# Three spectral products issued one gate/up product later in a float32 GLU plus spectral-filter kernel

## The chip, the cores and the metric

One NeuronCore of one Trainium2 chip runs the whole program. The metric is the device time of one execution in microseconds (us). The engines named below are TensorE (PE, with PEld for its weight loads), VectorE (DVE), ScalarE (ACT), GpSimd (POOL, nearly unused here) and SyncE (SP, whose queue issues almost all transfers).

## The reference

The input x has 2048 rows of 576 float32 values. It is normalised row by row, and the result is the sum of three terms:

```python
xn = _layernorm(x)                                   # per row, no scale or shift
A  = irfft2(rfft2(xn) * (w_r + 1j * w_i))            # 2-D over (2048, 576)
B  = (sigmoid(xn @ w_gate) * (xn @ w_up)) @ w_down   # 576 -> 4608 -> 576
out = x + A + B
```

All of it is wanted to nearly float32 accuracy.

## The kernel before, in words

TensorE multiplies operands that are rounded to a shorter float32 form. To keep the accuracy, the kernel cuts each operand in two parts: a high part, which is a rounded copy made by ACT, and a low part, the source minus the high part, made by DVE. A product is then three matmuls: high by high, low by high, high by low. This "rounding into two parts" stands ahead of every product.

**The GLU part.** The rows are worked in two pairs of 1024 (p = 0 and 1), and the 4608 hidden features in 36 blocks of 128. One block of one pair is a *unit* u. A unit computes gate and up for two row chunks by a seven-product scheme (the names A11, S1, T1 and so on are its sums). Each of the seven *gate/up products* (function `made`, issued by `prod`, L700) is seven matmuls of 128x128 by 128x512 into one of the PSUM banks pA, pB and pE. ACT and DVE empty those banks: L778 copies pA into pB, L785 and L791 copy pB to v, L788 and L796 apply the sigmoid. The down projection runs beside it, as groups of twelve (later six) matmuls of 128x288, tile ps (L1050), that DVE (L984) or ACT (L1032) adds to or copies into accumulators. The last blocks use tile po (L839) instead.

**The spectral part** runs inside the second pair, in three stages of 16 steps each; every step is a Python generator.

- `phase1b(t)`: product pd (14 matmuls, L527), a rounding of its result into ah and al (four ACT and four DVE instructions of 64x290, L535 and L536), product pa (6 matmuls, L542), a copy x1 to SBUF by ACT (L544), a store to DRAM.
- `phase2(i)`: a load x2, its rounding into x2h (ACT, L560) and x2l (DVE, L561), product pb (6 matmuls, L566), two swapped copies sw by ACT (L568, L569), the multiplication with the complex weight on DVE (L572 to L574), a rounding into zh (ACT) and zl (DVE), both by the helper `split` (L242, L243), product pc (6 matmuls, L582), a copy u by ACT (L584), a store.
- `phase3(t)`: a load u3, its rounding into uh (ACT, L603) and ul (DVE, L604), product py (6 matmuls, L609), copies, transposes pz (L622, L625), another rounding, product pe (12 matmuls, L640), and the addition of the result to the output rows. For t below 8 these rows are loaded into tile fin (L595) and stored from it (L653).

**What sets the order.** After each gate/up product the function `beside(i)` of the main loop advances the down projection by a piece (`rounds`) and then calls `aside()`, which advances every running generator by one `yield`. So one `yield` is one gate/up product. A table starts a phase1b step every 4.1 products, then a phase2 step every 4.1, then a phase3 step every 4.5 (U1, U2, U3). This gives the program order. From it a list scheduler makes, when the program is built, one fixed order for each engine and each queue, by its own estimates of when operands will be there; only instructions marked `keep_in_program_order` are held. On the chip every engine then works its own list from the front and waits where an operand or a buffer is not ready.

**Buffers.** pd, pa, pb, pc, py, pz, pe, ps and po all take their PSUM space from one pool of two buffers (`pair`, tag pp, two banks each). Banks pA and pB exist once, pE twice. ah, al, x2h, x2l, zh, zl, uh and ul have one buffer each; fin has two.

The main loop calls `aside` from `beside`:

```python
next(rounds, None)
turn(2 if u + 1 < NF else 1)
if u > NF + G:
    active.extend(b() for b in begin.pop(step, []))
    step += 1
    aside()
```

Of the kernel before, what the change touches and what calls it, by code (L numbers as in the profile page):

```python
# [163 lines left out]
def spectral_glu_kernel(ctx: ExitStack, tc: tile.TileContext, x, xt, xg, ri, w_in, w_down, out):  # L164
# [3 lines left out]
    def f32(ap):  # L168
        return ap.bitcast(F32)

    def load_r(dst, src):
        nc.sync.dma_start(f32(dst), src)
# [3 lines left out]
    def pair(name):  # L176
        return ps.tile([P, 2, 512], F32, tag="pp", name=name, bufs=2)
# [63 lines left out]
    def split(hi, lo, src, eng=None):  # L241
        nc.scalar.activation(hi, src, AF.Copy)  # L242
        (eng or nc.vector).tensor_tensor(lo, src, f32(hi), op=OP.subtract)  # L243
# [255 lines left out]
    def phase1b(t):  # L499
        pool, cf = R["pool"], R["cf"]  # L500
        xs = pool.tile([P, 2, KT + 1, P], F32, tag="xs", name=f"xs{t}", bufs=2)
        nc.sync.dma_start(xs.rearrange("p h k s -> p (h k s)"), xt[t])
        am = pool.tile([P, 2, 2, P], F32R, tag="am", name=f"am{t}", bufs=2)
        load_r(am, con["am"][:, t * 4 * P:(t + 1) * 4 * P].rearrange("p (a h m) -> p a h m", a=2, h=2))
        yield
        yield
        yield
        yield
        eo = pool.tile([P, 2, KT + 1, P], F32, tag="eo", name=f"eo{t}")
        tc.keep_in_program_order(nc.vector.tensor_tensor(eo[:, 1], xs[:, 0], xs[:, 1], op=OP.subtract))  # L510
        nc.vector.tensor_tensor(eo[:, 0], xs[:, 0], xs[:, 1], op=OP.add)
        fh = pool.tile([P, 2, KT + 1, P], F32R, tag="fh", name=f"fh{t}")
        fl = pool.tile([P, 2, KT, P], F32R, tag="fl", name=f"fl{t}")
        nc.scalar.activation(fh, eo, AF.Copy)
        nc.vector.tensor_tensor(fl, eo[:, :, :KT], f32(fh[:, :, :KT]), op=OP.subtract)
        r = slice(REM, 2 * REM)
        nc.vector.tensor_tensor(fh[r, :, KT], eo[r, :, KT], f32(fh[r, :, KT]), op=OP.subtract)
        yield
        yield
        pd = pair(f"pd{t}")  # L520
        for e in range(2):
            steps = []
            for k in range(2):
                steps += [(fh[:, e, k, :], cf[:, e, k, :]), (fl[:, e, k, :], cf[:, e, k, :]), (fh[:, e, k, :], cf[:, e, 2 + k, :])]
            steps.append((fh[:KR, e, KT, :], cf[:KR, e, 4, :]))
            for n, (l, r) in enumerate(steps):
                nc.tensor.matmul(pd[:, e, :NQ], l, r, start=n == 0, stop=n == len(steps) - 1)  # L527
        ah = pool.tile([P, 2, NQ], F32R, tag="ah", name=f"ah{t}", bufs=1)
        al = pool.tile([P, 2, NQ], F32R, tag="al", name=f"al{t}", bufs=1)
        for sl in range(2):  # L530
            for ci in range(2):
                o = slice(ci * N1, (ci + 1) * N1)
                i = slice(sl * N1, (sl + 1) * N1)
                v, r = pd[i, ci, :NQ], rstd[i, t:t + 1]
                nc.scalar.activation(ah[o, sl, :], v, AF.Copy, scale=r)  # L535
                nc.vector.scalar_tensor_tensor(al[o, sl, :], v, r, f32(ah[o, sl, :]), op0=OP.mult, op1=OP.subtract)  # L536
        yield
        yield
        pa = pair(f"pa{t}")
        for sl in range(2):  # L540
            for n, (h, m) in enumerate(((0, ah), (0, al), (1, ah))):
                nc.tensor.matmul(pa[:, sl, :NQ], am[:, sl, h, :], m[:, sl, :], start=n == 0, stop=n == 2)  # L542
        x1 = pool.tile([P, 2, NQ], F32, tag="x1", name=f"x1{t}", bufs=1)
        nc.scalar.activation(x1, pa[:, :, :NQ], AF.Copy)  # L544
        nc.sync.dma_start(sc1[2 * t * P:(2 * t + 2) * P].rearrange("(j p) n -> p j n", j=2), x1)

    def phase2(i):
        pool, bm, zz = R["pool"], R["bm"], R["zz"]
        kl = 2 * i
        x2 = pool.tile([P, 2, NQ], F32, tag="x2", name=f"x2{i}", bufs=2)  # L550
        nc.sync.dma_start(x2, sc1.rearrange("(p kl) n -> p kl n", kl=N2)[:, kl:kl + 2])
        w = pool.tile([P, 2, 2, NQ], F32, tag="ri", name=f"ri{i}", bufs=2)
        nc.sync.dma_start(w.rearrange("p a j n -> p (a j n)"), ri[i])
        wr, wi = w[:, 0], w[:, 1]
        yield
        yield
        yield
        h = pool.tile([P, 2, NQ], F32R, tag="x2h", name=f"x2h{i}")
        l = pool.tile([P, 2, NQ], F32R, tag="x2l", name=f"x2l{i}")
        tc.keep_in_program_order(nc.scalar.activation(h, x2, AF.Copy))  # L560
        nc.vector.tensor_tensor(l, x2, f32(h), op=OP.subtract)  # L561
        yield
        pb = pair(f"pb{i}")
        for j in range(2):
            for n, (k, m) in enumerate(((0, h), (0, l), (1, h))):
                nc.tensor.matmul(pb[:, j, :NQ], bm[:, k, :], m[:, j, :], start=n == 0, stop=n == 2)  # L566
        sw = pool.tile([P, 2, NQ], F32, tag="sw", name=f"sw{i}")
        nc.scalar.activation(sw[:N1], pb[N1:, :, :NQ], AF.Copy, scale=-1.0)  # L568
        nc.scalar.activation(sw[N1:], pb[:N1, :, :NQ], AF.Copy)  # L569
        z = pool.tile([P, 2, NQ], F32, tag="z", name=f"z{i}")  # L570
        t2 = pool.tile([P, 2, NQ], F32, tag="t2", name=f"t2{i}")
        nc.vector.tensor_tensor(z, wr, pb[:, :, :NQ], op=OP.mult)  # L572
        nc.vector.tensor_tensor(t2, wi, sw, op=OP.mult)
        nc.vector.tensor_tensor(z, z, t2, op=OP.add)  # L574
        zh, zl = zz[i % len(zz)]
        split(zh, zl, z)
        yield
        yield
        pc = pair(f"pc{i}")
        for j in range(2):  # L580
            for n, (k, m) in enumerate(((2, zh), (2, zl), (3, zh))):
                nc.tensor.matmul(pc[:, j, :NQ], bm[:, k, :], m[:, j, :], start=n == 0, stop=n == 2)  # L582
        u = pool.tile([P, 2, NQ], F32, tag="u", name=f"u{i}", bufs=2)
        nc.scalar.activation(u, pc[:, :, :NQ], AF.Copy)  # L584
        nc.sync.dma_start(sc2.rearrange("(p kl) n -> p kl n", kl=N2)[:, kl:kl + 2], u)

    def phase3(t):
# [14 lines left out]
        ul = pool.tile([P, 2, NQ], F32R, tag="ul", name=f"ul{t}")  # L602
        tc.keep_in_program_order(nc.scalar.activation(uh, u, AF.Copy))  # L603
        nc.vector.tensor_tensor(ul, u, f32(uh), op=OP.subtract)  # L604
        yield
        py = pair(f"py{t}")
        for sl in range(2):
# [493 lines left out]
    for (base, rate), phase, n in ((U1, phase1b, NT), (U2, phase2, N2 // 2), (U3, phase3, NT)):  # L1101
        for t in range(n):
            begin.setdefault(1 + base + int(t * rate), []).append(lambda t=t, phase=phase: phase(t))
# [458 lines left out]
```

## Time and profile before

| what | value |
|---|---|
| median of 3 runs | 1386.56 us (1386.12 to 1386.62) |
| the profiled execution | 1386.0 us |
| its span, first to last instruction | 1384.1 us |
| PE, share of the span | 99% (7688 matmuls) |
| PEld | 87% |
| DVE | 76% |
| ACT | 54% |
| granted TensorE clock | 1.000 |
| matmuls of pa, pc and py together | 288 |

The profiled execution is 1.9 us longer than its span, and 0.56 us below the median of the runs. The spectral stages lie at 697 to 897 us (phase1b), 915 to 1110 us (phase2) and 1110 to 1360 us (phase3) of the span. A row of a timeline gives start, duration, engine, line, operation, tiles, shapes and count, and in brackets the idle time of the engine before it with what ended it. A row of waits gives who waited for whom: the sum in us, how many times, the longest.

### The profile page before, as it was taken

What the parts mean: (1) busy time and instruction counts of PE and PEld (TensorE: products, weight loads), DVE (VectorE), ACT (ScalarE), POOL (GpSimd) and SP (SyncE); (2) the same over time, 40 slices, a digit from 0 to 9 for tenths busy, and PEclk for the clock granted to TensorE, in tenths of its full rate; (3) what the DMA queues carried; (4) which work ended last, traced back from release to release, by engine and by line L of the source; (5) the groups of instructions that cost most, each with busy time, mean ns of one, the idle gap of its engine ahead of it and who ended that gap; (6) DMA issues with size and microseconds to landing.
All of it is one profiled execution on the core that took longest, in us unless ns stands there. A gap on an engine that the chain in (4) does not pass through costs nothing. (4 is left out here: it accounts for less than half of the span.)

```text
span 1384.1 us, 20414 instructions
## 1 busy us (share of the span) xinstructions
PE 1371.5 (99%) x7688; PEld 1204.6 (87%) x7688; DVE 1046.0 (76%) x1523; ACT 742.0 (54%) x1180; POOL 3.3 (0%) x5
## 2 busy tenths in 40 slices
PE   8999999999999999999999999999999999999998
PEld 6888888888888888988888889988888889889888
DVE  7978889787878787999357467667767657777895
ACT  6644767777676777743155545445544434343432
POOL 0000000000000000000000000000000000000000
PEclk9999999999999999999999999999999999999999
DMA  7567776767667676686787767688888788676643
GB/s 256 207 252 285 269 313 263 274 265 272 261 258 264 247 264 247 262 271 221 258 260 232 220 211 239 199 276 271 270 269 268 234 259 256 216 238 184 195 149 86
DMA packets 120657, 337.05 MB, mean 244 GB/s; under 512 B 12560, under 2 KB 29744, under 8 KB 115824
## 3 DMA queue, kind: packets, MB, share of 16 engines
q1 hardware_dynamic: 119568, 334.44, 70.3%
q8 instruction: 61, 1.00, 0.3%
q10 hardware_dynamic: 992, 1.31, 0.3%
q14 instruction: 36, 0.29, 0.1%
HBM read 203.99 MB, written 131.71 MB: 243 GB/s over the span
## 5 line engine op out<-in xcount | busy, mean ns | idle before, releaser
L700 PE MATMUL pB<-X,w 128*128 128x512 f32 x1484 | 380.1, 393 | 0.6 <-ACT v L791 0.4
L1050 PEld LDWEIGHTS ps<-wf,hs 128*128 128x128 f32 x2436 | 348.0, 188 | 19.1 <-DVE acc L984 0.5
L1050 PE MATMUL ps<-wf,hs 128*128 128x288 f32 x2436 | 360.6, 295 | 0.1
L700 PEld LDWEIGHTS pB<-X,w 128*128 128x128 f32 x1484 | 269.2, 188 | 52.4 <-ACT v L791 3.3
L700 PE MATMUL pE<-X,w 128*128 128x512 f32 x1064 | 271.8, 392 | 0.0
L700 PE MATMUL pA<-X,w 128*128 128x512 f32 (+1 forms) x1006 | 256.4, 390 | 0.5 <-ACT X L476 0.2
L700 PEld LDWEIGHTS pE<-X,w 128*128 128x128 f32 x1064 | 194.1, 188 | 35.8 <-DVE ys L793 0.4
L700 PEld LDWEIGHTS pA<-X,w 128*128 128x128 f32 x1006 | 181.7, 188 | 34.1 <-ACT g L788 1.1
L971 DVE TENSOR_TENSOR hs<-ys,hs 128x1024 fp32r<-128x1024 f32 (+1 forms) x105 | 124.7, 1187 | 50.8 <-ACT hs L968 49.8
L968 ACT ACTIVATE hs<-ys 128x1024 fp32r<-128x1024 f32 (+1 forms) x105 | 108.0, 1028 | 48.4 <-PE ps L1050 41.7
L282 ACT ACTIVATE w<-raw 128x768 fp32r<-128x768 f32 (+1 forms) x106 | 100.3, 948 | 54.0 <-DVE raw L306 28.7
L815 DVE TENSOR_TENSOR ys<-ys,g 128x1024 f32<-128x1024 f32 x67 | 81.9, 1223 | 3.8 <-DVE ys L813 0.5
L284 DVE TENSOR_TENSOR w<-raw,w 128x512 fp32r<-128x512 f32 (+1 forms) x106 | 81.7, 771 | 2.5 <-ACT w L282 2.3
L793 DVE TENSOR_TENSOR ys<-v,pE 128x512 f32<-128x512 f32 x68 | 46.5, 684 | 44.0 <-ACT v L791 43.2
L796 ACT ACTIVATE g<-pB 128x512 f32<-128x512 f32 x68 | 40.5, 596 | 67.3 <-PE pB L700 67.2
L778 ACT ACTIVATE pB<-pA 128x512 f32<-128x512 f32 x68 | 39.6, 583 | 64.5 <-PE pA L700 64.4
L964 DVE TENSOR_TENSOR ys<-ys 128x1024 f32<-128x1024 f32 (+1 forms) x60 | 71.1, 1185 | 0.6
L839 PEld LDWEIGHTS po<-wb,hp 128*128 128x128 f32 x468 | 65.1, 188 | 2.6 <-ACT hp L877 0.4
L984 DVE TENSOR_TENSOR acc<-acc,ps 128x576 f32<-128x576 f32 x55 | 41.3, 751 | 34.2 <-PE ps L1050 33.9
L839 PE MATMUL po<-wb,hp 128*128 128x288 f32 x468 | 67.0, 295 | 0.0
L984 DVE TENSOR_TENSOR qs<-qs,ps 128x576 f32<-128x576 f32 x62 | 46.5, 750 | 25.2 <-PE ps L1050 25.1
L813 DVE TENSOR_TENSOR ys<-v,pE 128x512 f32<-128x512 f32 x67 | 45.8, 683 | 22.7 <-PE pE L700 22.1
(187 smaller groups left out, 1540.2 us busy)
## 6 DMA issues: line engine op xcount, KB each, us to landing
w<-wsp SPq DMA_DIRECT2D x246, 320.0 KB, 3.7
wsp<-w SPq DMA_DIRECT2D x34, 2240.0 KB, 7.2
wf<-fsp SPq DMA_DIRECT2D x105, 288.0 KB, 4.3
fsp<-wf SPq DMA_DIRECT2D x98, 288.0 KB, 3.4
raw<-in_w SPq DMA_DIRECT2D x34, 768.0 KB, 6.9
ri<-in_ri SPq DMA_DIRECT2D x16, 580.0 KB, 5.0
dt<-in_wd SPq DMA_DIRECT2D x32, 288.0 KB, 5.9
xs<-in_xt SPq DMA_DIRECT2D x16, 384.0 KB, 5.6
```

The costliest lines, as they stand in the source:

```text
L282: placed(nc.scalar.activation(o[:, :, :3, :], src, AF.Copy))
L284: placed(nc.vector.tensor_tensor(o[:, :, 3:, :], src[:, :, :KT, :], f32(o[:, :, :KT, :]), op=OP.subtract))
L700: strictly(nc.tensor.matmul(bank[:, cols], w[:, sw, :], X[:, x, sx, cols], start=start and j == 0, stop=stop and j == len(steps) - 1, skip ...
L793: nc.vector.tensor_tensor(y1, v[:, 1], bank["E"], op=OP.add)
L813: nc.vector.tensor_tensor(place(u, 0), v[:, 0], bank["E"], op=OP.add)
L815: nc.vector.tensor_tensor(h, h, g, op=OP.mult)
L839: nc.tensor.matmul(pd[b], l, r, start=start, stop=stop)
L964: nc.vector.tensor_tensor(o, at(a), at(b), op=op)
L968: nc.scalar.activation(hs[:, :, 0], o, AF.Copy)
L971: nc.vector.tensor_tensor(hs[:, :, 1], o, f32(hs[:, :, 0]), op=OP.subtract)
L984: nc.vector.tensor_tensor(o, a, b, op=op)
L1050: nc.tensor.matmul(pd[:, s], h[:, g, a, m], w[:, g, b], start=q == 0 and not seeded, stop=q == len(parts_) - 1, skip_group_check=seeded)
```

## The change

In each of the three phases one `yield` is added ahead of the product that stands behind a rounding, so that pa, pc and py are issued one gate/up product later than before, and what follows them in the same step moves along. Nothing is added or removed on any engine. The lines below the first edit have numbers higher by one, two or three in the changed kernel (L542 becomes L543, L582 becomes L584, L609 becomes L612).

```diff
@@ phase1b, behind the rounding into ah and al
         yield
         yield
+        yield
         pa = pair(f"pa{t}")
@@ phase2, behind split(zh, zl, z)
         yield
         yield
+        yield
         pc = pair(f"pc{i}")
@@ phase3, behind the rounding into uh and ul
         nc.vector.tensor_tensor(ul, u, f32(uh), op=OP.subtract)
         yield
+        yield
         py = pair(f"py{t}")
```

All engines keep their order up to the first pa. From there the scheduler's lists differ. Three places follow; the numbers behind the tile names only tell tiles of one name apart.

**TensorE, first step of phase1b (t = 0).** Before:

```order
L700 MATMUL pE_6422<-X,w_6055 128x512 x7
L700 MATMUL pB_6421<-X,w_6055 128x512 x7
L542 MATMUL pa_6476<-ah_6449,am_6359 128x290
L542 MATMUL pa_6476<-al_6450,am_6359 128x290
L542 MATMUL pa_6476<-ah_6449,am_6359 128x290
L700 MATMUL pA_6420<-X,w_6055 128x512 x3
L542 MATMUL pa_6476<-ah_6449,am_6359 128x290
L700 MATMUL pA_6420<-X,w_6055 128x512 x2
L542 MATMUL pa_6476<-al_6450,am_6359 128x290
L542 MATMUL pa_6476<-ah_6449,am_6359 128x290
L700 MATMUL pA_6420<-X,w_6055 128x512 x2
```

In the changed kernel:

```order
L703 MATMUL pE_6422<-X,w_6055 128x512 x7
L703 MATMUL pB_6421<-X,w_6055 128x512 x7
L703 MATMUL pA_6420<-X,w_6055 128x512 x7
L543 MATMUL pa_6497<-ah_6449,am_6359 128x290
L543 MATMUL pa_6497<-al_6450,am_6359 128x290
L543 MATMUL pa_6497<-ah_6449,am_6359 128x290 x2
L543 MATMUL pa_6497<-al_6450,am_6359 128x290
L543 MATMUL pa_6497<-ah_6449,am_6359 128x290
L703 MATMUL pB_6421<-X,w_6055 128x512 x7
```

The six matmuls of pa stood among the seven of a gate/up product; now they stand together behind it.

**TensorE, eleventh and twelfth step of phase2 (pc of step 10, pb of step 11).** Before:

```order
L700 MATMUL pE_9474<-X,w_6055 128x512
L582 MATMUL pc_9616<-zh,bmt 128x290
L700 MATMUL pE_9474<-X,w_6055 128x512 x6
L1050 MATMUL ps_7_5_0_9614<-wf_7_5_9432,hs_7_5_9543 128x288 x2
L582 MATMUL pc_9616<-zl,bmt 128x290
L582 MATMUL pc_9616<-zh,bmt 128x290 x2
L582 MATMUL pc_9616<-zl,bmt 128x290
L582 MATMUL pc_9616<-zh,bmt 128x290
L1050 MATMUL ps_7_5_0_9614<-wf_7_5_9432,hs_7_5_9543 128x288 x10
L700 MATMUL pA_9658<-X,w_6055 128x512 x7
L566 MATMUL pb_9673<-x2h_9652,bmt 128x290
L566 MATMUL pb_9673<-x2l_9653,bmt 128x290
```

In the changed kernel:

```order
L703 MATMUL pE_9474<-X,w_6055 128x512 x7
L1053 MATMUL ps_7_5_0_9614<-wf_7_5_9432,hs_7_5_9543 128x288 x12
L584 MATMUL pc_9642<-zh,bmt 128x290
L584 MATMUL pc_9642<-zl,bmt 128x290
L584 MATMUL pc_9642<-zh,bmt 128x290 x2
L584 MATMUL pc_9642<-zl,bmt 128x290
L584 MATMUL pc_9642<-zh,bmt 128x290
L703 MATMUL pA_9658<-X,w_6055 128x512 x7
L567 MATMUL pb_9673<-x2h_9652,bmt 128x290
L703 MATMUL pE_9660<-X,w_6055 128x512 x2
L567 MATMUL pb_9673<-x2l_9653,bmt 128x290
```

pc stands together behind the group ps, only one gate/up product (seven matmuls) ahead of the next pb; and pb, which was in one piece, now has two matmuls of pE behind its first.

**ScalarE, the same place.** Before:

```order
L242 ACTIVATE zh<-z_9571 128x580
L560 ACTIVATE x2h_9652<-x_9578 128x580
L796 ACTIVATE g_9470<-pB_9473 128x512
L584 ACTIVATE u_9623<-pc_9616 128x580
L778 ACTIVATE pB_9659<-pA_9658 128x512
```

In the changed kernel:

```order
L242 ACTIVATE zh<-z_9571 128x580
L799 ACTIVATE g_9470<-pB_9473 128x512
L586 ACTIVATE u_9649<-pc_9642 128x580
L561 ACTIVATE x2h_9652<-x_9578 128x580
L781 ACTIVATE pB_9659<-pA_9658 128x512
```

The rounding x2h of step 11 stood two places ahead of the copy u of step 10, which waits for pc; now it stands behind that copy. It does so in 14 of the 15 steps that follow another.

## The prediction

> **What bounds the kernel now.** I read the page first: the share of each engine, the clock, the chain that ended last.
>
> ```profile
> PE 1371.5 (99%) x7688; PEld 1204.6 (87%) x7688; DVE 1046.0 (76%) x1523; ACT 742.0 (54%) x1180; POOL 3.3 (0%) x5
> PEclk9999999999999999999999999999999999999999
> PE 45%; DVE 1%; ACT 1%; issue 0%; DMA 0%; ACTq 0%
> ```
>
> TensorE is the bound: 99% busy at full clock, and the chain that ended last is almost all PE. The change takes no matmul away, so it can only change the time in which PE stands still between matmuls. That the busy share leaves little room is not the whole story, because the row of a matmul covers its way through the array and overlaps the next one. A short standstill therefore hides inside "busy", and the starts must be read instead. So the next view is the timeline around one pa (step 5 of phase1b), and for comparison step 12:
>
> ```profile
> 757.22 1.77 PE L700 MATMUL pA<-X,w 128*128 128x512 f32 x7
> 762.00 1.30 PE L700 MATMUL pB<-X,w 128*128 128x512 f32 x5
> 763.19 0.65 ACT L1032 ACTIVATE qs<-ps 128x576 f32<-128x576 f32 x1
> 763.20 0.53 DVE L536 SCALAR_TENSOR_TENSOR al<-pd,rstd,ah 64x290 fp32r<-64x290 f32 x1 [0.56 <-ACT ah L535]
> 763.89 0.19 PEld L542 LDWEIGHTS pa<-ah,am 128*128 128x128 f32 x1 [1.02 <-ACT qs L1032]
> 763.89 0.40 PE L542 MATMUL pa<-ah,am 128*128 128x290 f32 x1 [0.60 <-ACT qs L1032]
> 764.13 0.29 PE L542 MATMUL pa<-al,am 128*128 128x290 f32 x1
> ...
> 848.12 1.79 PE L700 MATMUL pE<-X,w 128*128 128x512 f32 x7
> 852.97 0.29 PE L542 MATMUL pa<-ah,am 128*128 128x290 f32 x1
> 853.10 0.30 PE L542 MATMUL pa<-al,am 128*128 128x290 f32 x1
> 853.77 1.78 PE L700 MATMUL pA<-X,w 128*128 128x512 f32 x7
> 855.39 1.75 PE L1050 MATMUL ps<-wf,hs 128*128 128x288 f32 x12
> 856.97 1.30 PE L700 MATMUL pB<-X,w 128*128 128x512 f32 x5
> ```
>
> Undisturbed, seven gate/up matmuls take 855.39 - 853.77 = 1.62 us (0.23 each), a group ps 1.58, a matmul of pa 0.13. In step 5 five gate/up matmuls started at 762.00, so pa could have started at 763.15 and started at 763.89: 0.74 lost. Then the stalled matmul takes 764.13 - 763.89 = 0.24 where 0.13 is usual, another 0.11. Together 0.85, against an idle time of PEld of 1.02: the weight load runs ahead when nothing stops it, so a wait costs PE the idle time of PEld less about 0.15. With that rule the waits of PEld, by stage (697 to 737, 737 to 850, 915 to 1110 and 1110 to 1380 us), give the loss:
>
> ```profile
> PEld pa L542 <- ACT ah L535: 1.4, 3, 0.6
> PEld pa L542 <- DVE al L536: 0.3, 1, 0.3
> ...
> PEld pa L542 <- ACT qs L1032: 1.5, 3, 1.0
> PEld pa L542 <- PE ps L1050: 1.5, 3, 0.7
> PEld pa L542 <- DVE qs L984: 0.7, 1, 0.7
> PEld pa L542 <- issue: 0.5, 1, 0.5
> PEld pa L542 <- DVE al L536: 0.4, 1, 0.4
> ...
> PEld pc L582 <- DVE zl L243: 3.3, 11, 0.4
> PEld pc L582 <- ACT zh L242: 2.6, 9, 0.4
> ...
> PEld py L609 <- DVE acc L984: 0.7, 1, 0.7
> PEld py L609 <- DVE ul L604: 0.3, 1, 0.3
> ```
>
> pa: 6.3 us in 13 waits, so 6.3 - 13 x 0.15 = 4.4. pc: 5.9 in 20 waits, 5.9 - 3.0 = 2.9. py: 1.0 in 2 waits, 0.7. That is 8.0 us in all, and it is the most that the three edits can take away directly.
>
> **The change, part by part.** No instruction is added; the terms are waits that go, waits that stay and waits that come. The sum goes against the profiled execution, 1386.0 us; it lies 0.6 below the median of the three runs, 1386.56, and I add that at the end.
>
> *pa.* What pa waits for is late by its distance from pd. In step 5 pd ends where the next product begins, 757.22, and the last al ends at 763.20 + 0.53 = 763.73, 6.5 us later; this is the step with the greatest delay before pa (longest wait 1.0). In step 12 pd ends at 848.12 and pa starts at 852.97 without a wait, so there 4.85 is enough. The new list has three products between pd and pa in the steps 0 to 2 (3 x 1.62 = 4.9, and no ps there that loads ACT), three products and one ps in 3 to 9 (6.4), three and two ps in 10 to 15 (8.0). Only step 5 still misses, by about 0.1, and pays the 0.11 on top; I leave 0.3 for it and others like it. Gain 4.1. Behind pa nothing comes too early: the copy x1 and the next pd use the two PSUM buffers, and pd stands 1.6 (steps 11 to 15) to 3.2 us behind pa, where the copy of 128x580 takes 0.65. Bounds: 4.4 (all gone) and 1.8 (the waits on qs and ps, 3.7 in 7, stay; see the first rival).
>
> *pc.* The chain from pb to the parts of z, at step 10:
>
> ```profile
> 1034.92 1.78 PE L700 MATMUL pB<-X,w 128*128 128x512 f32 x7
> 1039.32 0.69 ACT L242 ACTIVATE zh<-z 128x580 fp32r<-128x580 f32 x1
> 1040.94 0.76 DVE L243 TENSOR_TENSOR zl<-z,zh 128x580 fp32r<-128x580 f32 x1
> 1042.62 1.48 PE L1050 MATMUL ps<-wf,hs 128*128 128x288 f32 x10
> 1042.82 0.66 ACT L584 ACTIVATE u<-pc 128x580 f32<-128x580 f32 x1 [1.75 <-PE pc L582]
> ...
> L560 ACT ACTIVATE x2h<-x 128x580 fp32r<-128x580 f32 x16 | 10.8, 677 | 0.0
> L561 DVE TENSOR_TENSOR x2l<-x,x2h 128x580 fp32r<-128x580 f32 x16 | 12.1, 758 | 5.8 <-ACT x2h L560 5.8
> ```
>
> pb ends at 1034.92, zh is there 5.1 us later and zl at 1041.70, 6.8 later. The new list puts pc three products and one ps behind pb (6.4) in most steps, 8.0 in some. zh is always in time. zl is needed one matmul later, at 6.4 + 0.13, and at a step as slow as this one would still be about 0.3 late. I take that for a quarter of the steps: 4 x (0.1 to 0.3 + 0.11) = 0.7 stays. Gain 2.2; bounds 2.9 and 1.0.
>
> *pb, the new wait.* The rounding x2h of the next step now stands on ACT behind u, which waits for pc. From the rows: pc ends at 1042.62 (the next matmul's start), u at 1042.82 + 0.66 = 1043.48, x2h would end at 0.68 more, 1044.16, x2l 0.76 after that, about 1044.95: 1.55 and 2.35 us behind pc. Queued behind x2h on ACT are the copies of the gate/up banks, and behind x2l on DVE the additions of ps, but both can run only when PE has gone on. Up to step 10 pb stands a product and a ps, 3.2 us, behind pc: hidden. In the steps 11 to 15 it is a single product, 1.62: x2h comes in the last moment, and x2l at 2.35 meets a matmul that, with the two or three fillers, is due at about 1.62 + 0.13 + 0.46 = 2.2, its weight load 0.13 sooner. I take 0.3 to 0.4 for each (0.2 late, 0.11 for the stalled matmul), 1.5 for five. Bounds: 0, if x2h starts as u ends and the fillers cover the rest; 4.3, if each costs what the worst wait of the trace cost, 0.85.
>
> *py and its followers.* Of 0.7 lost, 0.3 was for ul, now a product earlier and gone. The other wait was for a PSUM buffer that DVE empties in L984, and that meets py wherever py stands. pz and pe move along with new neighbours. I take a gain of 0.3; bounds +0.7 and -0.85 (one such wait more).
>
> *Queues.* The stores of x1 and u and those of fin move a product later on SP; the loads of w and wf stand around them. Their cover is worked out at the third rival; the sum takes zero.
>
> Sum: 4.1 + 2.2 - 1.5 + 0.3 = 5.1 us. 1386.0 - 5.1 = 1380.9 by the profiled execution, and with the 0.6 that the median stands above it 1381.5; the small waits beside pd (one of 0.5 us for fh) have a good chance to go with the others, so I say **1381.2 us**.
>
> **Rivals.** *A: the pairs are short, not the time.* Seven of the 13 waits of pa (qs 1.5 and 0.7, ps 1.5: 3.7 us) end with what empties or fills the two PSUM buffers, not with ah or al. If the new place of pa meets the same shortage, 3.7 - 7 x 0.15 = 2.6 us of the gain stays away: 1383.8. For it: the row of step 5, where L1032, not al, ends the wait. Against it: L1032 stands behind the four roundings on ACT there, so both end together, and both are past when pa comes 0.6 us later; steps 11 to 15 with the same two buffers have no wait at all. The Trainium skill (Perfetto Trace Analysis, Optimization Strategy) says that the same gap repeating on the engine that should be saturated can mean that there is too little PSUM for the next tile. By that rule it would come out like this rival; the trace bears it out in 7 of 13 waits.
>
> *B: pb takes back what pc gains.* If ACT or DVE is busy when pc ends (an hs copy of 1.0 us or its DVE partner of 1.2 us), each of the five late pb costs 0.85 instead of 0.3: 4.3 instead of 1.5, so 1381.2 + 2.8 = 1384.0. For it: in the old list x2h of those steps ran mostly ahead of pc. Against it: x2h follows u with nothing between, and two or three fillers stand there. The Trainium skill (PSUM — Partial Sum Buffer, Engine vs sequencer instructions) says that ScalarE's queue is strictly first in, first out, so that x2h cannot pass u; no row of this trace shows one passing another. Were it otherwise, the 1.5 would fall away and the sum would be 1379.7.
>
> *C: slower, by the SP queue.*
>
> ```profile
> 1195.36 0.38 SPq L653 DMA_DIRECT2D out<-fin  x1
> 1199.00 0.32 SPq L595 DMA_DIRECT2D fin<-spill  x1
> 1199.41 0.86 SPq L947 DMA_DIRECT2D wf<-fsp  x2
> ...
> 1215.49 1.79 PE L1050 MATMUL ps<-wf,hs 128*128 128x288 f32 x12
> ...
> DMA to landing us min/median/max: 2.7/3.6/5.1
> ...
> SPq L595 <- DMA out<-fin: 9.0, 6, 2.2
> ```
>
> The load of fin waits for the store of the fin two steps earlier, and everything behind it on SP waits with it. That store now comes a product and a ps (3.2 us) later, so the six waits could grow from 9.0 to 28 us. The wf behind one of them is issued at 1199.41, lands by about 1204 and is used two items later, at the earliest at 1215.49: 11 us of cover. Slower it gets from the point where a wait on SP is longer than that; each of the six would then hold PE for what is over. At 2.2 us over (the longest of these waits) it costs 13: 1394. The waits would have to grow fivefold, which is why I give it little.
>
> *D: no difference.* The standstills reappear elsewhere: PE's list is fixed, pA and pB are single banks, and new neighbours make new waits on their copies. Then 1386, from 8.0 gained and about 8 new.
>
> **How the numbers follow.** Forecast, 1379 to 1383.5: 0.68. A: 0.13. B: 0.10. C: 0.03. D: 0.06. What a measurement of this kernel can tell from no change is about 0.2%, 2.8 us, so faster means below 1383.8. The forecast lies below it, A and B on the line, half each side: faster 0.68 + 0.11 = 0.79; same 0.12 + 0.06 less 0.01 for a D that ends beyond = 0.17; slower 0.04. Range: the lower end takes all 8.0 gone and pb at 0, 1386.56 - 8.0 = 1378.5, the upper reaches over A and B, 1384.5.
>
> **What would show it.** In the profile after: the PEld waits of pa fall from 6.3 to below 1 us and those of pc from 5.9 to below 2; the matmul rows of pa stand as one block with distances of 0.13; a new row of PEld pb waiting for ACT x2h or DVE x2l, with 4 to 8 waits and 1 to 2.5 us, in the last third of phase2; PE, its matmul count and the clock as before. If the waits of pa on qs and ps stay, it was A; if the row of pb shows over 4 us, B; if ps waits for a DMA of wf, C. The prediction is wrong if the time is above 1384.5 or below 1378.5, and in its reasons if the gain does not sit at 697 to 850 us (about 4) and 915 to 1110 (about 1).

## The result and the profile after

The changed kernel takes **1378.93 us** (median of 6 runs, 1378.50 to 1379.43) against 1386.57 for the kernel before in the same session: ratio 0.9946, 95% interval 0.9933 to 0.9958. That is 7.6 us faster. The prediction said 1381.2, with a range from 1378.5 to 1384.5; the time lies inside it, 0.4 us above its lower end. The execution profiled below took 1378.5 us, with a span of 1376.5.

First the page of the changed kernel: the engines and the clock.

```profile
PE 1365.8 (99%) x7688; PEld 1205.7 (88%) x7688; DVE 1045.7 (76%) x1523; ACT 743.1 (54%) x1180; POOL 3.3 (0%) x5
PEclk9999999999999999999999999999999999999999
```

The matmul count and the clock are as before and PE's share still says 99%, as the prediction had warned: the 7.6 us do not show in it. They show in the starts. The first matmul of pd (step 0), of pb (step 0) and of pb (step 15), and the first of the last group, stand at the same places of PE's order in every kernel of this document. From the timelines of before (first four rows) and after (last four):

```profile
700.80 0.30 PE L527 MATMUL pd<-cf,fh 128*128 128x290 f32 x1
917.90 0.30 PE L566 MATMUL pb<-x2h,bmt 128*128 128x290 f32 x1
1091.45 0.29 PE L566 MATMUL pb<-x2h,bmt 128*128 128x290 f32 x1
1378.61 0.97 PE L839 MATMUL po_B<-wb,hp 128*128 128x288 f32 x6
...
700.82 0.29 PE L527 MATMUL pd<-cf,fh 128*128 128x290 f32 x1
912.90 0.30 PE L567 MATMUL pb<-x2h,bmt 128*128 128x290 f32 x1
1084.13 0.30 PE L567 MATMUL pb<-x2h,bmt 128*128 128x290 f32 x1
1371.01 0.95 PE L842 MATMUL po_B<-wb,hp 128*128 128x288 f32 x6
```

Three stages follow by subtraction. Stage 1 (first pd to first pb) took 217.1 us and now takes 212.1: 5.0 gained. Stage 2 (first pb to last pb) took 173.6 and now takes 171.2: 2.3 gained (173.55 less 171.23). The rest took 287.2 and now takes 286.9: 0.3. Of the 7.6 us, 7.3 lie in the first two.

The waits of PE's weight loads after, at 697 to 905, at 905 to 1110 and (py and pe only) at 1110 to 1380 us:

```profile
PEld pB L703 <- ACT v L794: 0.6, 1, 0.6
PEld pd L527 <- DVE fl L515: 0.2, 1, 0.2
...
PEld pb L567 <- DVE x2l L562: 1.4, 5, 0.3
PEld pc L584 <- DVE zl L243: 0.3, 1, 0.3
...
PEld pe L643 <- DVE z3l L243: 0.8, 2, 0.4
PEld pe L643 <- ACT z3r L633: 0.6, 2, 0.4
PEld py L612 <- DVE acc L987: 0.5, 1, 0.5
PEld py L612 <- DVE qs L987: 0.2, 1, 0.2
...
PEld pe L643 <- issue: 0.2, 1, 0.2
```

No wait of pa is left, where there were 6.3 us in 13. One wait of pc is left, where there were 20. The row of pb is new, with as many waits as predicted and at the small end of what was predicted for their sum. The timeline around step 5 of phase1b shows pa as the prediction wanted it, six matmuls with distances of 0.13 and no bracket of idle time (rows of DVE first, then PE):

```profile
759.95 0.53 DVE L536 SCALAR_TENSOR_TENSOR al<-pd,rstd,ah 64x290 fp32r<-64x290 f32 x1
...
754.84 1.77 PE L703 MATMUL pA<-X,w 128*128 128x512 f32 x7
761.20 0.29 PE L543 MATMUL pa<-ah,am 128*128 128x290 f32 x1
761.33 0.30 PE L543 MATMUL pa<-al,am 128*128 128x290 f32 x1
```

pd ends at 754.84, the last al at 760.48, pa starts at 761.20: the operand is 0.7 us early. Before, in this step, it was there 6.5 us behind pd; now 5.64, because DVE's order changed with it: before, an eo (0.55 us) stood ahead of the first al and a part of fh (0.41 us) ahead of the second, and now both come later.

### The profile page after: what moved, and what is told of

The parts are those of the page before. It is cut to its first block, busy times and chain, and to the rows that moved or that the text cites. A ratio compares the mean times of both kernels' runs of the same rounds, so it can differ in the third digit from the quotient of the medians.

```text
span 1376.5 us, 20419 instructions
## 1 busy us (share of the span) xinstructions
PE 1365.8 (99%) x7688; PEld 1205.7 (88%) x7688; DVE 1045.7 (76%) x1523; ACT 743.1 (54%) x1180; POOL 3.3 (0%) x5
## 4 chain that ended last, share of the span: by engine, by line
PE 91%; DVE 7%; issue 1%; ACT 1%; DMA 0%; DVEq 0%; ACTq 0%
PE pB L703 23%; PE ps L1053 22%; PE pE L703 16%; PE pA L703 15%; PE po L842 5%; PE pd L527 2%; PE pe L643 2%; PE pb L567 1%; PE py L612 1%; PE pc L584 1%; PE pa L543 1%; DVE acc L851 1%; DVE w L284 0%; PE pz L625 0%; PE b L1129 0%
```

## The experiments

The theory: **a product waits because its rounded operand is late, and one gate/up product more is enough**; behind pc the new order on ACT takes a little back at pb. The rivals are those of the prediction, above all A (two PSUM pairs are short). Each run is compared with the kernel before on the same chip (1386.52, 1386.73 and 1386.38 us in three sessions). The table gives medians of 5 runs (6 in its first row, 11 for pc alone and for the two runs with pd early), and the three stages of each profiled execution.

| kernel | median us | less than before | stage 1 | stage 2 | rest |
|---|---|---|---|---|---|
| before | 1386.57 | | 217.1 | 173.6 | 287.2 |
| changed kernel, run again | 1378.74 | 7.6 | 212.0 | 171.2 | 286.9 |
| pa alone | 1381.31 | 5.2 | 212.0 | 173.8 | 286.7 |
| pc alone | 1384.05 | 2.5 | 217.0 | 171.5 | 286.8 |
| pa and pc, not py | 1378.59 | 7.9 | 212.0 | 171.2 | 287.0 |
| pd early, from step 1 | 1384.18 | 2.3 | 214.8 | 173.9 | 286.7 |
| pd early, from step 3 | 1384.09 | 2.6 | 214.8 | 173.9 | 286.8 |
| changed, pa two later | 1381.25 | 5.5 | 213.7 | 171.4 | 286.8 |
| changed, pc two later | 1379.77 | 7.0 | 212.0 | 171.7 | 286.8 |
| changed, x2 earlier | 1378.09 | 8.6 | 212.0 | 170.4 | 286.8 |
| the same, py as before | 1378.14 | 8.2 | 212.0 | 170.4 | 287.0 |
| x2 earlier, pe later | 1377.30 | 9.1 | 212.1 | 170.4 | 286.0 |

The start of the first pd, which none of these edits moves in PE's order, varies from 700.6 to 702.6 us between these executions; that is why differences below 1 us are read in the stages.

### One edit at a time

The first two kernels have one of the three added lines each, the third has two.

```diff
+        yield
         pa = pair(f"pa{t}")
```

> Only pa stands one product later; pc and py as before. The theory of late operands (pa waits only because ah and al are not there yet): all of the gain at 697 to 897 us, about 5.0 of the 7.6 us, so 1386.6 - 5.0 = 1381.6; the 13 waits of PEld at pa (6.3 us) gone, the waits at pc as before (about 5.9 us in 20). The rival that the gain comes from the rearranged list as a whole, not from pa's own waits: less than half of it here, above 1383.5.

> Only pc stands one product later. The theory: pc's waits fall from 5.9 us in 20 to about 0.3 in 1, and x2h, now behind u on ScalarE, makes about 5 waits of pb with 1.4 us; net gain 2.2 us, 1384.4. The rival that pb takes back what pc gains: 1386, no difference. That both would add up with the run of pa alone to the whole change (less about 0.5 for py) is part of the theory.

> pa and pc one product later, py as before. The theory that py is worth 0.3 to 0.5 us: 1379.3, slower than the whole change (1378.9) by that little. The rival that the move of py costs (new waits of py on accumulators, pz and pe with new neighbours): 1378.4 or less, faster than the whole change.

pa alone: 1381.31 us, ratio 0.9963 (0.9951 to 0.9976). pc alone: 1384.05, 0.9982 (0.9973 to 0.9991). Their gains of 5.2 and 2.5 add up to 7.7; both together gave 7.9, and all three edits 7.6. So the parts are independent, and the place of the gain is as the theory had it: in the table each edit shortens its own stage, and the others stay within 0.5 us. The waits at 905 to 1110 us, with pa alone (first two rows) and with pc alone:

```profile
PEld pc L583 <- DVE zl L243: 3.5, 11, 0.5
PEld pc L583 <- ACT zh L242: 2.9, 10, 0.4
...
PEld pb L566 <- DVE x2l L561: 1.6, 5, 0.4
PEld pc L583 <- DVE zl L243: 0.3, 1, 0.3
```

21 waits of pc against one, and the five waits of pb come with the edit at pc. On py neither theory was confirmed: without its edit the time was 1378.59 where 1379.3 was the one expectation and 1378.4 or less the other; the ranges of the runs overlap (1378.36 to 1379.41 without, 1378.50 to 1379.43 with).

### Late operands or short pairs

This kernel leaves pa at about its old place and puts everything ahead of it in the step one product earlier. (The place is not quite the same: in step 5 pa now follows the group ps directly, where five matmuls of pB stood between.)

```diff
+        if t:
+            yield
         pa = pair(f"pa{t}")
...
-            begin.setdefault(1 + base + int(t * rate), []).append(lambda t=t, phase=phase: phase(t))
+            begin.setdefault(1 + base + int(t * rate) - (phase is phase1b and t > 0), []).append(lambda t=t, phase=phase: phase(t))
```

> pa stays where it was before among its neighbours (the same ps ahead of it), and everything ahead of it in the step (loads, sums, rounding, pd) is issued one product earlier from step 1 on, so the distance from pd to pa is that of the changed kernel. Late operands: the waits of pa go just as with pa moved, but for step 0, which is left as it was: about 0.3 us less gain than with pa moved alone, 1381.9. Two PSUM pairs short at pa's old place: the waits of pa on qs and ps (3.7 us in 7, 2.6 us of time) stay, 1384.3 or above. pd may wait for its own rounding if the load of xs is late: then PEld waits at pd beyond the 0.5 us of before, and the time says less.

1384.18 us: by the time alone this is the rival's number (1384.3 or above), not the 1381.9 of late operands. But the caveat of the expectation came true in part: a load of xs was late, though the wait that it made was at pa and not at pd. The worst wait of pa, of step 1, in the timeline (rows of DVE, ACT, PE):

```profile
718.93 0.56 DVE L511 TENSOR_TENSOR eo<-xs 128x384 f32<-128x384 f32 x1 [1.18 <-DMA xs<-in_xt]
719.52 0.52 DVE L536 SCALAR_TENSOR_TENSOR al<-pd,rstd,ah 64x290 fp32r<-64x290 f32 x1
...
720.08 0.50 ACT L535 ACTIVATE ah<-pd,rstd 64x290 fp32r<-64x290 f32 x1 [2.24 <-DVE al L536]
...
720.63 0.40 PE L544 MATMUL pa<-ah,am 128*128 128x290 f32 x1 [1.41 <-ACT ah L535]
```

An addition eo of step 2 waited 1.18 us for the load of xs; behind it on DVE stood an al of step 1, the last ah waited for that, and pa for the ah. From 737 us on no wait of pa was left. The same edit from step 3 on (`t > 2` in both places) keeps the first loads out of it:

> As the run with pd issued earlier, but only from step 3 on, so that the first loads of xs, which were late there, stay as before. Late operands: in steps 3 to 10 the kernel before lost 3.3 us at pa; all of it goes though pa keeps its old neighbours, 1386.5 - 3.3 = 1383.2, and no wait of PEld at pa is left at 745 to 850 us. Two PSUM pairs short at pa's old place: the waits on qs and ps, which lie in these steps, stay with 2.6 us, 1385.8.

1384.09 us, ratio 0.9983 (0.9974 to 0.9991): 2.6 gained, nearer to 3.3 than to 0.7. What decides is the stretch from 755 to 850 us (steps 5 to 10), where before every wait of pa is put down to what fills or empties the pairs. Before, its waits of PEld at pa:

```profile
PEld pa L542 <- PE ps L1050: 1.5, 3, 0.7
PEld pa L542 <- ACT qs L1032: 1.3, 2, 1.0
PEld pa L542 <- DVE qs L984: 0.7, 1, 0.7
```

With pd early there is none in this stretch, and PEld's only wait in it is one of pB (0.5 us). So 3.5 us of waits went by an earlier pd, and what rival A forecast, that they stay, has fallen. It does not follow that pa had waited for its operand. Step 7 of the kernel before (rows of DVE, then PEld):

```profile
785.69 0.51 DVE L536 SCALAR_TENSOR_TENSOR al<-pd,rstd,ah 64x290 fp32r<-64x290 f32 x1
...
788.36 0.53 DVE L536 SCALAR_TENSOR_TENSOR al<-pd,rstd,ah 64x290 fp32r<-64x290 f32 x1 [0.56 <-ACT ah L535]
788.96 0.19 PEld L542 LDWEIGHTS pa<-ah,am 128*128 128x128 f32 x1 [0.67 <-PE ps L1050]
```

The first three matmuls of pa read the halves of ah and al that the first two roundings write; the second of them ended at 786.20. But the first weight load of pa started only 0.07 us behind the fourth al. That one writes the other half, and it is the last to read pd, whose two PSUM banks pa gets in this step. So pa waited for a pair, and the roundings themselves empty it; the "PE ps" of the row had ended before. Steps 4, 8 and 9 show the same 0.07. In steps 3, 5, 6 and 10 pa gets the banks of the group ps ahead of it, and its first load started 0.05 to 0.06 us behind the end of qs, which empties them. In all eight steps the operands of its first three matmuls had been there for 1.8 us or more. These eight waits are 4.1 us of PEld. The other five (2.1 us, in steps 0 to 3) came at the fourth or fifth matmul and ended 0.05 us behind an ah or al: those are late operands.

The run with pd early cannot separate the two, because the same roundings that make the operand empty pd's pair. It also changes which pair is taken: in steps 4 to 10 pa now always gets that of pd. What a third pair would have saved was not measured.

Two steps did not follow: at 745 to 850 us the one wait of pa is

```profile
PEld pa L544 <- DVE al L536: 0.4, 1, 0.4
...
748.44 1.22 DVE L973 TENSOR_TENSOR hs<-ys,hs 128x1024 fp32r<-128x1024 f32 x1
749.69 0.53 DVE L536 SCALAR_TENSOR_TENSOR al<-pd,rstd,ah 64x290 fp32r<-64x290 f32 x1
750.27 0.40 PE L544 MATMUL pa<-ah,am 128*128 128x290 f32 x1
```

That is step 4. pd ended at 741.96 there, so al was still not there 8.2 us later, because DVE's order put an hs ahead of it. Step 3 lost 0.5 us, too, where the profile names no releaser; its last al ended at 738.21 and pa started at 738.31. Together the two steps lost 0.95 us by the starts, and with them the 2.35 us that stage 1 gained (217.1 to 214.75) would be the 3.3 of the expectation. So the distance from pd is the measure only as long as DVE's and ACT's orders stay the same.

### One more product

```diff
         yield
+        yield
         pa = pair(f"pa{t}")
```

> The changed kernel with pa one more product later, right ahead of the next pd. The theory that one product made pa's operands early enough: nothing left to gain, 1378.9 within 0.4, no waits of pa. The rival that pa's place, not the time behind pd, was what mattered: another difference of 1 us or more, in either sign; if pa and pd back to back run out of PSUM pairs, new waits of pd on x1 or of ps on al, 0.3 to 0.85 each in up to 15 steps, 1383 or more.

1381.25 us (1380.73 to 1381.46): 2.3 slower than the changed kernel. By the stages it is 1.8, of which 1.6 in stage 1; 0.7 more lies ahead of the first pd of the profiled execution (701.5 against 700.8), where the edit changes nothing. pa has no wait, but pd, now right behind it, has new ones (737 to 850 us):

```profile
PEld pd L527 <- ACT x L546: 1.7, 2, 1.0
PEld pd L527 <- ACT qs L1036: 0.7, 4, 0.2
...
PE pd L527 <- DVE qs L988: 0.6, 1, 0.6
```

x1 (shown as x) and qs empty the pairs. At the two longest of these waits (at 755.15 and 831.88) the last to end was DVE's addition of ps (L988), 0.12 us ahead of the load. So here, too, the pairs are short, now at pd. It cost less than the 1383 that the expectation gave for this rival, as only two steps lose more than 0.3 us at pd by the starts (0.55 and 0.83). For pc the second product has the same sign:

> The changed kernel with pc one more product later: it now stands beside the next pb, with 1 to 7 matmuls between them, and x2h is back ahead of u in most steps. Theory of late operands: pc's last 0.4 and pb's 0.7 go, 1377.8. The rival that the pairs are short: pb and pc hold both, so that the next ps or pb waits for u or sw, 0.3 to 0.85 in ten steps or more, 1382 to 1387.

1379.77 us (1379.39 to 1379.84). pc's last wait went, as expected, but pb, now beside it, has more:

```profile
PEld pb L567 <- issue: 2.1, 8, 0.4
PEld pb L567 <- DVE x2l L562: 0.6, 2, 0.3
PEld pb L567 <- DVE qs L988: 0.2, 1, 0.2
```

The theory's 1377.8 missed, and so did the rival's 1382: by the starts pb lost 1.9 us here against 0.7 in the changed kernel, and pc gained back 0.4; stage 2 is 0.5 longer. (In the profiled execution 1.1 us more lies ahead of the first pd, 702.0 against 700.8, where the edit changes nothing.) Two of the waits are for x2l. For eight of the nine others the profile names nothing, but DVE's rows show what ended them. The first of them, in step 1:

```profile
924.57 0.76 DVE L988 TENSOR_TENSOR qs<-qs,ps 128x576 f32<-128x576 f32 x1 [0.91 <-PE ps L1054]
...
925.44 0.19 PEld L567 LDWEIGHTS pb<-x2h,bmt 128*128 128x128 f32 x1 [0.22 <-issue]
```

In all nine DVE's addition of ps, which empties the pair that pb gets, ended 0.05 to 0.12 us ahead of the load, and x2h had been there for 1.2 us or more. So here as well the wait is for a pair.

### pb and x2h

The steps of phase2 from 1 on begin one product earlier, and pb is held where it was:

```diff
         yield
+        if i:
+            yield
         pb = pair(f"pb{i}")
...
-            begin.setdefault(1 + base + int(t * rate), []).append(lambda t=t, phase=phase: phase(t))
+            begin.setdefault(1 + base + int(t * rate) - (phase is phase2 and t > 0), []).append(lambda t=t, phase=phase: phase(t))
```

> The changed kernel, and from step 1 on the steps of phase2 begin one product earlier with pb held where it is: x2h and x2l are rounded one product earlier, ahead of u on ScalarE instead of behind it. The theory that pb waits only because x2h stands behind u: the 5 waits of PEld at pb (1.4 us, 0.7 us on PE) go, 1378.9 - 0.7 = 1378.2. The rival that the wait at pb is DVE's (x2l behind other work), whatever place x2h has: they stay, 1378.9. If x2 lands too late or zh is pushed back by x2h, pc waits again: above 1379.

1378.09 us, ratio 0.9940 (0.9926 to 0.9953), and stage 2 takes 170.4 instead of 171.2 us. The row of pb is gone; the only wait left at 905 to 1110 is

```profile
PEld pc L586 <- ACT zh L242: 0.3, 1, 0.3
```

So pb waited because x2h stood behind u, and that cost 0.8 us. With py put back as well:

> The changed kernel with x2 rounded one product earlier and with py back at its old place. Theory that the move of py is worth nothing that can be measured: 1378.1 within 0.4, like the run with x2 earlier. That it is worth the 0.3 of the prediction: 1378.4 or more. That it costs: 1377.7 or less.

1378.14 us (1377.79 to 1378.43), where the changed kernel took 1378.74 (1378.39 to 1379.45) on the same chip:

> The changed kernel again, on the same chip as the two runs beside it, so that differences below 1 us can be read against it: 1378.9 within 0.4.

This kernel differs from the run with x2 earlier in py alone, and that one took 1378.09: py's place makes no difference that can be measured. With its place put back py has two waits, 0.7 us for the addition acc, with which DVE empties a pair, and 0.3 us for ul. With the edit the wait on ul is gone, and those for the emptying of a pair stay (0.7 us, now in two).

### pe, the next rounding

On top of the run with x2 earlier, pe comes one product later:

```diff
+        yield
         pe = pair(f"pe{t}")
```

> The changed kernel with x2 rounded one product earlier and with pe one product later behind its own rounding. The theory that what holds for pa and pc holds for pe: its four waits (1.4 us of PEld, about 0.7 us on PE) go, 1378.1 - 0.7 = 1377.4. The rival that pe's later place costs as much elsewhere, as it did when pa and pc moved by a second product (a pair that is held longer, the end of the last step): 1378.1 or more.

1377.30 us (1376.69 to 1378.05), ratio 0.9934 (0.9921 to 0.9946): it beats the changed kernel of the same session by 1.4 us, the ranges being apart, and has the lowest median here. Some of the 1.4 is x2's. The part of pe shows in the last stage, 286.0 instead of 286.8 us, where the waits of pe and pz are gone. Two new waits are py's (1.1 and 0.5 us of PEld). The longer one:

```profile
1133.98 1.12 DVE L651 TENSOR_TENSOR ev<-pe,od 128x432 f32<-128x432 f32 x2
1135.19 0.37 PE L614 MATMUL py<-uh,ai 128*128 128x290 f32 x1 [0.87 <-issue]
```

pe of the step before holds a pair until ev has read it; ev ends at 1135.10, and py starts 0.09 us later. It happens in two of 16 steps (in the other, too, ev ended 0.07 us ahead of the load), and the gain is larger.

## Why the prediction was right, and where its sizes were off

**What bounds the kernel**: right. PE bounds it, the starts of its matmuls show what "busy" hides, and the price of a wait as the idle time of PEld less about 0.15 us came out: the six waits of 755 to 850 us before (3.5 us) give 3.5 - 6 x 0.15 = 2.6, and by the starts pa lost 2.63 in these steps.

**pa**: right that the distance from pd decides, 4.1 predicted, 5.0 measured in stage 1. What pa waited for was read only in part. For the five waits in steps 0 to 3 it was ah or al, as the sum had it. For the eight at pa's first matmul it was a pair. Four of these ended with the last al, which empties pd's pair; three of the four stand in the prediction's rows as "PE ps". The other four ended with qs. The gain came all the same, as the prediction argued against A for step 5: by the new time the roundings and the qs behind them are past, and with them the pair is free. The 0.3 that was left for step 5 did not stay (its operand is now 0.7 us early, since DVE's order around it changed too), which makes 4.4; by the starts pa lost some 4.4 before and nothing after. Most of the other 0.6 are waits that the sum had only as a chance beside pd and did not price at all at the banks. Before, these stood at 697 to 905 us too; after, one of 0.2 at pd (on fl) is left of their kind:

```profile
PEld pd L527 <- ACT fh L514: 0.5, 1, 0.5
...
PEld pB L700 <- ACT pB L778: 0.3, 1, 0.3
PEld pA L700 <- ACT g L788: 0.2, 1, 0.2
```

**pc and pb**: mechanism right, sizes off. The net was predicted as 2.2 - 1.5 = 0.7 and measured as 2.3. With pb's wait taken away, stage 2 gains 173.6 - 170.4 = 3.1 (unrounded 173.55 - 170.44), a little above the upper bound of 2.9: all of pc's waits went but one, where four had been kept at 0.7 together. And the five waits of pb cost 0.8, not 1.5. Their number and their place, the last third of phase2, were right; x2l is there, as worked out, some 2.3 us behind pc. The term that was too large is the 0.3 to 0.4 for each. At the last of them

```profile
1083.96 0.76 DVE L562 TENSOR_TENSOR x2l<-x,x2h 128x580 fp32r<-128x580 f32 x1 [1.30 <-ACT x2h L561]
1084.13 0.30 PE L567 MATMUL pb<-x2h,bmt 128*128 128x290 f32 x1
1084.26 0.63 PE L703 MATMUL pA<-X,w 128*128 128x512 f32 x2
1084.78 0.40 PE L567 MATMUL pb<-x2l,bmt 128*128 128x290 f32 x1
1085.02 0.43 PE L567 MATMUL pb<-x2h,bmt 128*128 128x290 f32 x2
```

the second matmul was due at 1084.26 + 2 x 0.23 = 1084.72 and started at 1084.78: 0.06 late, and 0.11 more because it then took 1085.02 - 1084.78 = 0.24. The fillers cover nearly all of it; I had counted 0.2 late.

**py**: 0.3 predicted, none that can be measured. The reason was named (the wait for a pair meets py wherever it stands). So the terms for pa and for pc with pb were both too small, by 0.9 and 1.6 us: that is how the time came to lie near the lower end of the range. **Queues**: from the spectral stages on no wait for a transfer appears at PE in the profile after, and the waits of the load of fin for a store, which C let grow from 9.0 to 28 us, fell to 5.5 in five. Rival C has fallen.

**Rivals.** What A forecast, a gain of 2.6 us that stays away, did not come. Its reading of the waits was right, for eight of 13 where it counted seven; what it had wrong is that a later pa would meet the same shortage. The Trainium skill (Perfetto Trace Analysis, Optimization Strategy) reads the same gap repeating on the engine to be saturated as a sign that PSUM for the next tile may be short. The trace agrees at pa before (4.1 us), at pd behind a pa two products later, at pb behind a pc two products later and at py behind a later pe: there al, qs, acc and ev ended last, and they empty a pair. But with the number of pairs unchanged the waits at pa went by time alone. B needed 4.3 us at pb and got 0.8. D fell with the time.

## What to carry to other kernels

When an engine that is 99% busy stands still for fractions of a microsecond, ask for each such product how late its operand is, and how late the buffer that it writes to becomes free. Both can hang on the same chain, and then one move helps both: here one product of 1.6 us was enough, and a second cost 0.4 us (pc) and 1.8 us (pa) by the stages, because it met another product that needs the same buffers. The releaser that a profile names for a wait need not be what ended it: three waits of pa were put down to "PE ps" and ended 0.07 us behind the last al, and eight of pb were put down to nothing and ended with DVE's addition of ps. The ends of the rows just ahead of the wait, and which operands that very matmul reads, tell more. Look also at what the move pushes back in an in-order queue (x2h behind u): putting it ahead again was worth 0.8 us.

## What the runs showed of the hardware

A load that comes late at one engine is paid at another with nothing in between that looks slow: 1.2 us of an addition waiting for its transfer became 1.41 us of idle time at pa, handed on by the order of DVE's instructions (al behind eo). And the price of a very short wait is mostly not the wait: at pb's last step PE lost 0.06 us waiting and 0.11 us on the matmul that was stalled, which took 0.24 instead of 0.13.
